# Reordering the frequency-domain products by time block, and accumulating the inverse transforms per frequency half

## The chip, the core and the metric

The kernel runs on one core of one Trainium2 chip. The metric is the device time of one execution in microseconds (us), the median of several runs. A profile of one execution gives, beside this, the span from the first to the last instruction.

## The reference

For one sequence of L = 2048 tokens and D = 512 channels, the output mixes two branches with a gate per token:

```python
g = _sigmoid((x * gate_w).sum(-1, keepdims=True))
a = _A_ref(x, ...)      # state-space convolution, every channel by its own kernel K, plus x * Dskip
b = _B_ref(x, ...)      # x, and for the 2 tokens with the largest x @ w_r a feed-forward part added
return g * a + (1 - g) * b
```

The part that matters here is the convolution in `_A_ref`. It builds a kernel K of 2048 lags per channel and convolves along time by way of spectra:

```python
K = jnp.einsum("dn,dnl,dn->dl", Cc, P, dB).real
Kf = rfft2(pad(K)); Uf = rfft2(pad(up))
Yf = Uf * Kf[None, :, :, :]
y = irfft2(Yf)[:, :, 0, :L] + u * Dskip
```

## The kernel before, in words

The kernel cuts time into two blocks of 1024 tokens and the channels into two halves `h` of 256. All transforms are matrix products on TensorE (PE) with cosine and sine matrices, with 512 frequency pairs in 4 tiles `ft` of 128, a real and an imaginary `part`, and even and odd time steps kept apart (`par` in time, `pm` for the two frequencies that share a cosine). The stages around the change are these.

- `forward` (from L711 on, matmuls L736 and L738) transforms the two time blocks of x into the tile X.
- `kgen(h)` (matmuls L756, L769, L775) makes the convolution kernel of a channel half, and `kspec(h)` (matmuls L791) transforms it into KK[h], kernel block by kernel block, in two halves `qd` of the frequency tiles (tiles 0 and 1, then 2 and 3). ScalarE (ACT) or VectorE (DVE) copies each result out of PSUM (recorded under helper line L402).
- `products(h, qd)` (L797 to L826) multiplies spectra on DVE, all of it tensor-tensor work recorded under helper line L387. For one frequency half it does block 1 and then block 0 (the loop at L811). Block 1 of the output is X1·K0 + X0·K1 and takes six operations on 2048 columns (into the scratch tiles PA, PBb and PC), then four on 1024 columns; block 0 is X0·K0 and takes two on 2048 and four on 1024. Of the four, the first two (L820, L821) write the scratch tile YY, and the last two (L825, L826), here called the closing sums, write the result over X in place, first for pm = 0, then for pm = 1. PA, PBb, PC and YY exist once, so that one unit's operations follow the other's in the order in which the program states them, with only little overlap.
- `inverse(h)` (L830 to L861) goes over block 1, then block 0; in each over `par`, and in that over the time half `t2`. One PE operation is 16 matmuls (L841): two column groups `e` of 8 accumulating matmuls each, over all 4 frequency tiles and both parts, into one of 4 PSUM buffers of one bank. It therefore needs the products of both frequency halves. For h = 0, and for block 1 of h = 1, ACT scales the result by the gate into YA (two operations, recorded under L398), and after the second t2 one DVE operation of 1024 columns adds YA to U (L852, recorded under L387). For block 0 of h = 1, DVE does both in one operation per column group (L857, recorded under L394). After a block, four DMAs on the queue of SyncE (SP) write 128 KB each to the output (L860, recorded under L409).

The main program states these steps in this order: `kspec(0)`, `kgen(1)`, `products(0, 0)`, `products(0, 1)`, the load of the inverse matrices G (L898), `kspec(1)`, `inverse(0)`, `products(1, 0)`, `products(1, 1)`, `inverse(1)` (L894 to L903).

The order on each engine is not the order of the program text. `Prog.schedule` (L107) is a planner: among all operations whose predecessors are planned it takes the one with the earliest start, and among equals the one with the longest remaining path (`key = (st, -o.bl - o.prio)`, L143), with costs that the program gives each operation. Each engine then runs its list strictly in that order and waits on semaphores. A copy out of PSUM that may go to ACT or DVE (`EV`) is put on the one that the planner expects to be done first.

Of the kernel before, what the change touches and what calls it, by code (L numbers as in the profile page):

```python
# [13 lines left out]
ACTF = mybir.ActivationFunctionType  # L14
# [3 lines left out]
PE, ACT, DVE, POOL, SP = "pe", "act", "dve", "pool", "sp"  # L18
# [9 lines left out]
def dr(a, off, *dims):  # L28
    return bass.AP(a.tensor, off, [[s, c] for (s, c) in dims])
# [225 lines left out]
L, D, NS, NF = 2048, 512, 128, 1792  # L255
BLK, NBLK, HF, HC = 1024, 2, 2, 256
# [70 lines left out]
def bass_gated_mix__ssm_conv_s4__moe_arch_mod__prompt_kernel(nc, A_u, A_A_re, A_A_im, A_B_re, A_B_im, A_C_re, A_C_im, A_log_dt, A_Dskip,  # L327
# [24 lines left out]
    with ExitStack() as es:  # L352
# [25 lines left out]
        def nel(ap):  # L378
            r = 1
            for s, c in ap.ap[1:]:  # L380
                r *= c
            return r
        def tt_cost(o, a, b):
            fast = all(x.dtype == BF for x in (o, a, b)) and all(str(x.tensor.name).startswith("AR") for x in (a, b))
            return 0.157 + nel(o) * (0.52e-3 if fast else 1.04e-3)
        def TT(o, a, b, op, rd, wr, **k):
            return P.op(DVE, lambda h: h.tensor_tensor(out=o, in0=a, in1=b, op=op), rd, wr, cost=tt_cost(o, a, b), **k)  # L387
# [5 lines left out]
        def STT(o, a, sc, b, op0, op1, rd, wr, **k):  # L393
            return P.op(DVE, lambda h: h.scalar_tensor_tensor(out=o, in0=a, scalar=sc, in1=b, op0=op0, op1=op1), rd, wr, cost=0.16 + nel(o) * 1.25e-3, **k)  # L394
        def CP(o, a, rd, wr, **k):
            return P.op(DVE, lambda h: h.tensor_copy(o, a), rd, wr, cost=0.16 + nel(o) * 0.8e-3, **k)
        def AC(o, a, func, rd, wr, scale=1.0, bias=0.0, **k):
            return P.op(ACT, lambda h: h.activation(out=o, in_=a, func=func, scale=scale, bias=bias), rd, wr,  # L398
                        cost=0.185 + nel(o) * 0.833e-3 + (0.09 if not isinstance(scale, float) else 0), **k)
# [8 lines left out]
        def DMA(pairs, rd, wr, nbytes, eng=SP, **k):  # L408
            return P.op(eng, lambda h: [h.dma_start(o, i) for o, i in pairs], rd, wr, cost=0.5 * len(pairs), n=len(pairs), nbytes=nbytes, dma=True, **k)  # L409
# [12 lines left out]
        U = B("u", oA, 16 * KB)  # L422
        X = B("x", oB, 32 * KB)
        P.bufs.remove(X)
        XB = [[B("x%d%d" % (h_, k_), oB + (16 * h_ + 8 * k_) * KB, 8 * KB) for k_ in range(2)] for h_ in range(2)]
        xk = lambda h_, k_, *key: (XB[h_][k_], key)
# [26 lines left out]
        G = B("g", oF + 16 * KB, 16 * KB)  # L453
# [114 lines left out]
        MUL, ADD, SUB = ALU.mult, ALU.add, ALU.subtract  # L568
# [225 lines left out]
                        o = KK[h](0, 128, i * 4096 + part * 2048 + 2 * qd * 256, (1024, 2), (1, 512))  # L794
                        EV(o, pb(0, 128, 0, (512, 2), (1, 512)), [pb.buf], [(KK[h], (i, part, qd))])

        def products(h, qd):  # L797
            def xv(blk, part=None, pm=None):
                o = h * 8192 + blk * 4096 + 2 * qd * 256
                if part is None:  # L800
                    return X(0, 128, o, (2048, 2), (1024, 2), (1, 512))
                if pm is None:
                    return X(0, 128, o + part * 2048, (1024, 2), (1, 512))
                return X(0, 128, o + part * 2048 + pm * 1024, (1, 512))
            def kv(blk, part):
                return KK[h](0, 128, blk * 4096 + part * 2048 + 2 * qd * 256, (0, 2), (1024, 2), (1, 512))
            v4 = lambda b: b(0, 128, 0, (1024, 2), (512, 2), (1, 512))
            v1 = lambda b, part: b(0, 128, part * 1024, (1, 1024))
            kx = lambda blk: [xk(h, blk, part, pm, ft) for part in range(2) for pm in range(2) for ft in (2 * qd, 2 * qd + 1)]
            kk = lambda blk, part: [(KK[h], (blk, part, qd))]  # L810
            for blk in (1, 0):  # L811
                TT(v4(PA), xv(blk), kv(0, 0), MUL, kx(blk) + kk(0, 0), [PA])
                if blk == 1:
                    TT(v4(PC), xv(0), kv(1, 0), MUL, kx(0) + kk(1, 0), [PC])
                    TT(PA(0, 128, 0, (1, 2048)), PA(0, 128, 0, (1, 2048)), PC(0, 128, 0, (1, 2048)), ADD, [PA, PC], [PA])
                TT(v4(PBb), xv(blk), kv(0, 1), MUL, kx(blk) + kk(0, 1), [PBb])
                if blk == 1:
# [12 lines left out]
        def inverse(h):  # L830
            for blk in (1, 0):
                for par in range(2):
                    for t2 in range(2):
                        pb = ivb[ni[0] % 4]
                        ni[0] += 1
                        def iv(hh, blk=blk, par=par, t2=t2, pb=pb):
                            last = None
                            for e in range(2):
                                for c in range(8):
                                    part, ft = c % 2, c // 2  # L840
                                    last = hh.matmul(pb(0, 128, e * 256, (1, 256)), G(0, 128, ((par * 2 + part) * 4 + ft) * 512 + (2 * t2 + e) * 128, (1, 128)),  # L841
                                                     X(0, 128, h * 8192 + blk * 4096 + part * 2048 + (par * 4 + ft) * 256, (1, 256)), start=(c == 0), stop=(c == 7))
                            return last
                        P.op(PE, iv, [G] + [xk(h, blk, part, par, ft) for part in range(2) for ft in range(4)], [pb.buf], cost=16 * 0.11)
                        if h == 0 or blk == 1:
                            for e in range(2):
                                tb = blk * 8 + (2 * t2 + e) * 2 + par
                                AC(YA(0, 128, (2 * t2 + e) * 256 + par * 1024, (1, HC)), pb(0, 128, e * 256, (1, HC)), ACTF.Copy, [pb.buf, (SG, "g")], [(YA, (par, t2, e))], scale=SG(0, 128, 32 + tb, (1, 1)))
                            if t2 == 1:
                                tbs = [blk * 8 + s_ * 2 + par for s_ in range(4)]  # L850
                                u = U(0, 128, (blk * 8 + par) * D + h * HC, (2 * D, 4), (1, HC))
                                TT(u, u, YA(0, 128, par * 1024, (HC, 4), (1, HC)), ADD, [(YA, (par, a_, e)) for a_ in range(2) for e in range(2)] + [(U, ("x", tb)) for tb in tbs], [(U, ("o", tb, h)) for tb in tbs])  # L852
                            continue
                        for e in range(2):
                            tb = blk * 8 + (2 * t2 + e) * 2 + par
                            u = U(0, 128, tb * D + h * HC, (1, HC))
                            STT(u, pb(0, 128, e * 256, (1, 256)), SG(0, 128, 32 + tb, (1, 1)), u, MUL, ADD, [pb.buf, (SG, "g"), (U, ("x", tb))], [(U, ("o", tb, h))])  # L857
                for st in range(4):
                    tb = blk * 8 + st * 2
                    DMA([(dr(out, (1024 * blk + 256 * st) * D + h * HC, (2 * D, 128), (D, 2), (1, HC)), U(0, 128, tb * D + h * HC, (D, 2), (1, HC)))],  # L860
                        [(U, ("o", tb, h)), (U, ("o", tb + 1, h))], [], 131072, tag="final")  # L861
# [31 lines left out]
        tab2(1, (1, 1))  # L893
        kspec(0)  # L894
        kgen(1)
        products(0, 0)
        products(0, 1)
        DMA([(G(0, 128, 0, (1, 8192)), g_c[:, :])], [], [G], 2097152)  # L898
        kspec(1)
        inverse(0)  # L900
        products(1, 0)
        products(1, 1)
        inverse(1)  # L903

        P.span = P.schedule()
# [45 lines left out]
```

## Time and profile before

| | |
|---|---|
| time, median of 3 runs | 206.42 us (206.23 to 206.93) |
| span of the profiled execution | 203.5 us |
| median less span | 2.9 us |
| PE busy | 163.9 us (81%) |
| DVE busy | 171.3 us (84%) |
| ACT busy | 141.1 us (69%) |
| mean granted PE clock | 0.921 |

The page gives the profiled execution by its span; its own whole time is not listed apart from the three runs. Where a step below is worked out on the span, it is carried over to the median as a difference. Busy shares are means over stages with different limits, so the stage that holds the change, from about 150 us to the end, is to be read by itself: which engine waits there, and for whom.

### The profile page before, as it was taken

Reading aid. Unit: us, or ns where it says so; the run is one execution under the profiler, and the core shown is the slowest. Engines: PE = TensorE matmul, PEld = TensorE weight load, DVE = VectorE, ACT = ScalarE, POOL = GpSimd, SP = SyncE. Lnnn points to the kernel's source line nnn. Section 1 sums busy time; section 2 is a strip of 40 time slices with the busy share of each in tenths; the row PEclk is TensorE's granted clock in tenths of the full one; section 3 lists DMA queues with packets and bytes.
Section 4 is the critical chain, followed back from the end, with each engine's and each line's share of the span. In section 5 each row is a group of like instructions: output and inputs, shape, how many; then the busy total and the mean of one; then the engine's idle time right before and its main releaser. Section 6 shows DMA issues by size and latency. Waiting matters only on the chain.

```text
span 203.5 us, 3609 instructions
## 1 busy us (share of the span) xinstructions
PE 163.9 (81%) x1479; PEld 108.6 (53%) x1490; DVE 171.3 (84%) x281; ACT 141.1 (69%) x232; POOL 3.4 (2%) x7
## 2 busy tenths in 40 slices
PE   0084799999999999999984999509889999809992
PEld 0073544774344444466550387408668888607881
DVE  0579545699999999999489999999999999999152
ACT  2599999989999999699999946406636654401400
POOL 6000000000000000000000000000000000000000
PEclk9997579999999999999997599966999999985998
DMA  5998999149202022000498000000280000303033
GB/s 86 271 323 364 307 410 358 33 121 293 53 0 55 0 52 52 0 3 0 135 435 362 0 5 0 0 0 3 61 354 0 3 0 0 106 0 103 0 103 103
DMA packets 22097, 23.17 MB, mean 114 GB/s; under 512 B 13121, under 2 KB 19394, under 8 KB 21442
## 3 DMA queue, kind: packets, MB, share of 16 engines
q1 hardware_dynamic: 20738, 22.63, 33.8%
q10 hardware_dynamic: 1344, 0.33, 1.4%
q8 instruction: 11, 0.18, 0.4%
q14 instruction: 4, 0.03, 0.0%
HBM read 19.02 MB, written 3.15 MB: 109 GB/s over the span
## 4 chain that ended last, share of the span: by engine, by line
PE 63%; DVE 22%; ACT 7%; DMA 4%; issue 1%; SPq 1%; DVEq 0%
PE ps L736 28%; DVE AR L387 20%; PE ps L841 12%; PE ps L791 6%; PE ps L756 5%; ACT AR L402 4%; DMA AR<-in_A_u_dram 4%; PE ps L769 3%; ACT AR L398 3%; PE ps L738 2%; PE ps L711 2%; PE ps L625 1%; PE ps L700 1%; SPq L483 1%; PE ps L637 1%
## 5 line engine op out<-in xcount | busy, mean ns | idle before, releaser
L387 DVE TENSOR_TENSOR AR<-AR 128x1024 bf16<-128x1024 bf16 (+7 forms) x184 | 135.7, 797 | 12.5 <-DMA AR<-in_A_A_re_dram 6.8
L398 ACT ACTIVATE AR<-AR 128x512 bf16<-128x512 f32 (+4 forms) x84 | 59.5, 769 | 5.4 <-DVE AR L391 2.1
L402 ACT ACTIVATE AR<-ps 128x1024 bf16<-128x1024 f32 (+4 forms) x56 | 44.0, 811 | 25.5 <-PE ps L791 12.8
L736 PE MATMUL ps<-AR 128*128 128x512 bf16 x248 | 59.0, 388 | 0.8 <-issue 0.5
L736 PEld LDWEIGHTS ps<-AR 128*128 128x128 bf16 x256 | 25.3, 100 | 30.2 <-issue 2.7
L841 PE MATMUL ps<-AR 128*128 128x256 bf16 x256 | 31.1, 287 | 5.9 <-DVE AR L387 5.9
L398 ACT ACTIVATE AR<-ps,AR 128x256 bf16<-128x256 f32 (+1 forms) x40 | 20.4, 565 | 18.8 <-PE ps L841 18.8
L841 PEld LDWEIGHTS ps<-AR 128*128 128x128 bf16 x256 | 26.3, 103 | 10.2 <-DVE AR L387 6.2
L791 PE MATMUL ps<-AR 128*128 128x256 bf16 x224 | 26.1, 274 | 1.7 <-ACT AR L402 1.7
L791 PEld LDWEIGHTS ps<-AR 128*128 128x128 bf16 x224 | 21.7, 99 | 6.1 <-ACT AR L402 3.1
L406 ACT ACTIVATE AR<-AR 128x256 int32<-128x256 f32 (+1 forms) x50 | 21.1, 484 | 0.1
L756 PE MATMUL ps<-AR 128*128 128x84 bf16 x256 | 13.5, 213 | 7.9 <-DVE AR L387 7.6
L756 PEld LDWEIGHTS ps<-AR 128*128 128x128 bf16 x256 | 12.0, 105 | 11.1 <-DVE AR L387 7.9
L625 PE MATMUL ps<-AR 128*128 128x128 bf16 x64 | 6.3, 278 | 12.5 <-DMA AR<-in_A_u_dram 10.8
L391 DVE TENSOR_SCALAR AR<-AR 128x1024 int32<-128x1024 int32 (+4 forms) x24 | 13.2, 552 | 0.3
L625 PEld LDWEIGHTS ps<-AR 128*128 128x128 bf16 x64 | 5.4, 127 | 13.1 <-DMA AR<-in_A_u_dram 10.8
L402 DVE CAST AR<-ps 128x1024 bf16<-128x1024 f32 (+1 forms) x7 | 8.0, 1142 | 3.2 <-remote 1.7
L867 PE MATMUL ps<-AR 128*128 128x512 bf16 x13 | 6.4, 492 | 3.6 <-ACT AR L398 3.6
L868 PE MATMUL ps<-AR 128*128 128x512 bf16 x16 | 7.6, 474 | 0.2
L406 DVE TENSOR_SCALAR AR<-AR 128x256 int32<-128x256 f32 (+1 forms) x22 | 5.6, 296 | 1.9 <-ACT AR L398 1.8
L769 PE MATMUL ps<-AR 128*32 128x128 bf16 (+1 forms) x96 | 6.4, 383 | 0.5 <-ACT AR L402 0.5
L402 DVE COPY AR<-ps 128x1024 bf16<-128x1024 bf16 (+1 forms) x7 | 4.7, 686 | 1.7 <-PE ps L625 1.4
(36 smaller groups left out, 57.0 us busy)
## 6 DMA issues: line engine op xcount, KB each, us to landing
AR<-c_ksp SPq DMA_DIRECT2D x1, 3584.0 KB, 13.5
AR<-in_A_u_dram SPq DMA_DIRECT2D x2, 1024.0 KB, 8.4
AR<-c_fwd SPq DMA_DIRECT2D x1, 2048.0 KB, 8.0
AR<-c_fwdn SPq DMA_DIRECT2D x8, 256.0 KB, 4.4
AR<-c_inv SPq DMA_DIRECT2D x1, 2048.0 KB, 8.9
out_dram<-AR SPq DMA_DIRECT2D x16, 128.0 KB, 2.2
AR<-in_B_w_gate_dram SPq DMA_DIRECT2D x1, 1792.0 KB, 11.2
AR<-in_B_w_up_dram SPq DMA_DIRECT2D x2, 896.0 KB, 11.5
```

The lines of the kernel that those rows point to most:

```text
L387: return P.op(DVE, lambda h: h.tensor_tensor(out=o, in0=a, in1=b, op=op), rd, wr, cost=tt_cost(o, a, b), **k)
L391: return P.op(DVE, lambda h: h.tensor_scalar(out=o, in0=a, scalar1=s1, scalar2=None, op0=op0), rd, wr, cost=c, **k)
L398: return P.op(ACT, lambda h: h.activation(out=o, in_=a, func=func, scale=scale, bias=bias), rd, wr, cost=0.185 + nel(o) * 0.833e-3 + (0.09 ...
L402: return P.op((ACT, DVE), (lambda h: h.activation(out=o, in_=a, func=ACTF.Copy), lambda h: h.tensor_copy(o, a)), rd, wr, cost=(0.185 + n * ...
L406: return P.op((ACT, DVE), (lambda h: h.activation(out=o, in_=a, func=ACTF.Copy, scale=c), lambda h: h.tensor_scalar(out=o, in0=a, scalar1= ...
L625: last = h.transpose(bb(0, 128, db * 256 + t_ * 128, (1, 128)), U(0, 128, (2 * q + t_) * D + db * 128, (1, 128)), IDN(0, (1, 128)))
L736: last = h.matmul(o, w, U(0, 128, (blk * 8 + st * 2 + par) * D, (1, D)), start=(par + st == 0), stop=(par * 4 + st == 7 and blk == 0))
L756: last = hh.matmul(pb(0, 128, (g - b0) * 84, (1, 84)), TP[h][1 - part](0, 128, g * 128, (1, 128)), TQ[h][1 - part](0, 128, g * 84, (1, 84) ...
L769: last = hh.matmul(pb(32 * g, 32, c4, (256, njg), (4, 64)), lw, KA[h](0, 128, c4 + 4 * (8 * bk + g), (16, njg), (84, 64)), start=True, sto ...
L791: last = hh.matmul(pb(0, 128, n * 256, (1, 256)), KP(0, 128, u * 2048 + tau * 128, (1, 128)), KC[h](0, 128, jg * 256, (1, 256)), start=(k ...
L841: last = hh.matmul(pb(0, 128, e * 256, (1, 256)), G(0, 128, ((par * 2 + part) * 4 + ft) * 512 + (2 * t2 + e) * 128, (1, 128)), X(0, 128, h ...
L868: return h.matmul(pb(0, 128, c0, (1, D)), OHR(0, 128, tb * 128, (1, 128)), ZB(0, 128, D, (1, D)), start=False, stop=True)
```

## The change

Three things are changed.

1. `products(h, qd)` gets the list of blocks as an argument, and the main program calls it for block 1 of both frequency halves first, then for block 0 of both. The operations are the same.
2. In `inverse(h)` each PE operation of 16 matmuls becomes two of 8: `q = 0` accumulates frequency tiles 0 and 1 for all four pairs of `t2` and `par` into the four PSUM buffers, and `q = 1` accumulates tiles 2 and 3 on top. The matmuls are the same in number and shape; each operation now needs only its own frequency half. Only the first matmul into a bank starts a new accumulation.
3. Within a block the loop now goes over the time half `t2` outside and `par` inside, so that the DVE addition covers one time half (four neighbouring token tiles) in place of one parity. The ACT, DVE and DMA operations are the same in number and size.

The core of the diff:

```diff
-        def products(h, qd):
+        def products(h, qd, blks):
...
-            for blk in (1, 0):
+            for blk in blks:
...
             for blk in (1, 0):
-                for par in range(2):
+                bufs = {}
+                for q in range(2):
                     for t2 in range(2):
-                        pb = ivb[ni[0] % 4]
-                        ni[0] += 1
-                        def iv(hh, blk=blk, par=par, t2=t2, pb=pb):
-                            for e in range(2):
-                                for c in range(8):
-                                    part, ft = c % 2, c // 2
-                                    last = hh.matmul(..., start=(c == 0), stop=(c == 7))
-                        P.op(PE, iv, [G] + [xk(h, blk, part, par, ft) for part in range(2) for ft in range(4)], [pb.buf], cost=16 * 0.11)
+                        for par in range(2):
+                            if q == 0:
+                                bufs[t2, par] = ivb[ni[0] % 4]
+                                ni[0] += 1
+                            pb = bufs[t2, par]
+                            def iv(hh, blk=blk, par=par, t2=t2, pb=pb, q=q):
+                                for e in range(2):
+                                    for c in range(4):
+                                        part, ft = c % 2, 2 * q + c // 2
+                                        last = hh.matmul(..., start=(q + e + c == 0), stop=(q == 1 and e == 1 and c == 3))
+                            P.op(PE, iv, [G] + [xk(h, blk, part, par, ft) for part in range(2) for ft in (2 * q, 2 * q + 1)], [pb.buf], cost=8 * 0.11)
+                            if q == 0:
+                                continue
...
-                            if t2 == 1:
-                                tbs = [blk * 8 + s_ * 2 + par for s_ in range(4)]
-                                u = U(0, 128, (blk * 8 + par) * D + h * HC, (2 * D, 4), (1, HC))
-                                TT(u, u, YA(0, 128, par * 1024, (HC, 4), (1, HC)), ADD, ...)
+                                if par == 1:
+                                    tbs = [blk * 8 + 4 * t2 + k for k in range(4)]
+                                    u = U(0, 128, (blk * 8 + 4 * t2) * D + h * HC, (D, 4), (1, HC))
+                                    TT(u, u, YA(0, 128, t2 * 1024, (HC, 4), (1, HC)), ADD, ...)
...
-        products(0, 0)
-        products(0, 1)
+        for blks in ((1,), (0,)):
+            for qd in range(2):
+                products(0, qd, blks)
...
-        products(1, 0)
-        products(1, 1)
+        for blks in ((1,), (0,)):
+            for qd in range(2):
+                products(1, qd, blks)
         inverse(1)
```

More of the change, by code (lines that the diff above doesn't have):

```diff
@@ L831, in inverse @@
             for blk in (1, 0):
-                for par in range(2):
+                bufs = {}
+                for q in range(2):
                     for t2 in range(2):
-                        pb = ivb[ni[0] % 4]
-                        ni[0] += 1
-                        def iv(hh, blk=blk, par=par, t2=t2, pb=pb):
-                            last = None
-                            for e in range(2):
-                                for c in range(8):
-                                    part, ft = c % 2, c // 2
-                                    last = hh.matmul(pb(0, 128, e * 256, (1, 256)), G(0, 128, ((par * 2 + part) * 4 + ft) * 512 + (2 * t2 + e) * 128, (1, 128)),
-                                                     X(0, 128, h * 8192 + blk * 4096 + part * 2048 + (par * 4 + ft) * 256, (1, 256)), start=(c == 0), stop=(c == 7))
-                            return last
-                        P.op(PE, iv, [G] + [xk(h, blk, part, par, ft) for part in range(2) for ft in range(4)], [pb.buf], cost=16 * 0.11)
-                        if h == 0 or blk == 1:
+                        for par in range(2):
[4 more added lines that the diff above has]
+                            def iv(hh, blk=blk, par=par, t2=t2, pb=pb, q=q):
+                                last = None
+                                for e in range(2):
+                                    for c in range(4):
+                                        part, ft = c % 2, 2 * q + c // 2
+                                        last = hh.matmul(pb(0, 128, e * 256, (1, 256)), G(0, 128, ((par * 2 + part) * 4 + ft) * 512 + (2 * t2 + e) * 128, (1, 128)),
+                                                         X(0, 128, h * 8192 + blk * 4096 + part * 2048 + (par * 4 + ft) * 256, (1, 256)), start=(q + e + c == 0), stop=(q == 1 and e == 1 and c == 3))
+                                return last
+                            P.op(PE, iv, [G] + [xk(h, blk, part, par, ft) for part in range(2) for ft in (2 * q, 2 * q + 1)], [pb.buf], cost=8 * 0.11)
+                            if q == 0:
+                                continue
+                            if h == 0 or blk == 1:
+                                for e in range(2):
+                                    tb = blk * 8 + (2 * t2 + e) * 2 + par
+                                    AC(YA(0, 128, t2 * 1024 + (2 * e + par) * 256, (1, HC)), pb(0, 128, e * 256, (1, HC)), ACTF.Copy, [pb.buf, (SG, "g")], [(YA, (par, t2, e))], scale=SG(0, 128, 32 + tb, (1, 1)))
+                                if par == 1:
+                                    tbs = [blk * 8 + 4 * t2 + k for k in range(4)]
+                                    u = U(0, 128, (blk * 8 + 4 * t2) * D + h * HC, (D, 4), (1, HC))
+                                    TT(u, u, YA(0, 128, t2 * 1024, (HC, 4), (1, HC)), ADD, [(YA, (p_, t2, e)) for p_ in range(2) for e in range(2)] + [(U, ("x", tb)) for tb in tbs], [(U, ("o", tb, h)) for tb in tbs])
+                                continue
@@ L846, in inverse @@
                             for e in range(2):
                                 tb = blk * 8 + (2 * t2 + e) * 2 + par
-                                AC(YA(0, 128, (2 * t2 + e) * 256 + par * 1024, (1, HC)), pb(0, 128, e * 256, (1, HC)), ACTF.Copy, [pb.buf, (SG, "g")], [(YA, (par, t2, e))], scale=SG(0, 128, 32 + tb, (1, 1)))
-                            if t2 == 1:
-                                tbs = [blk * 8 + s_ * 2 + par for s_ in range(4)]
-                                u = U(0, 128, (blk * 8 + par) * D + h * HC, (2 * D, 4), (1, HC))
-                                TT(u, u, YA(0, 128, par * 1024, (HC, 4), (1, HC)), ADD, [(YA, (par, a_, e)) for a_ in range(2) for e in range(2)] + [(U, ("x", tb)) for tb in tbs], [(U, ("o", tb, h)) for tb in tbs])
@@ L853, in inverse @@
[L853 to L857, printed above, removed]
+                                u = U(0, 128, tb * D + h * HC, (1, HC))
+                                STT(u, pb(0, 128, e * 256, (1, 256)), SG(0, 128, 32 + tb, (1, 1)), u, MUL, ADD, [pb.buf, (SG, "g"), (U, ("x", tb))], [(U, ("o", tb, h))])
```

## The prediction, made before the changed kernel was run

> **What bounds the kernel now.** The page comes first, for the span and for the slices in which an engine is not full.
>
> ```profile
> span 203.5 us, 3609 instructions
> PE   0084799999999999999984999509889999809992
> DVE  0579545699999999999489999999999999999152
> PEclk9997579999999999999997599966999999985998
> ```
>
> A slice is 5.09 us. DVE is full from slice 23 to slice 36 and nearly empty in the last three. PE is full through slice 34, falls to 0 in slice 35 (178 to 183 us), and is full again to the end, in slice 36 at a clock of 0.5. So PE stands idle for DVE, restarts slowly, and is then the only full engine. The chain of waits for the last stretch and the table of waits say the same:
>
> ```profile
> 166.71 3.51 PE ps L841 x32
> 173.04 9.99 DVE AR L387 x12
> 183.08 16.68 PE ps L841 x128
> 199.78 0.48 DVE AR L394
> PE ps L841 <- DVE AR L387: 5.9, 1, 5.9
> ```
>
> All 128 inverse matmuls of the second channel half (`inverse(1)`) begin at 183.08, when DVE has block 1 complete in both frequency halves, and run without a break to 199.76. The end follows from them. A table of windows gives what each piece holds (window and length, then busy us and counts of PE, weight loads, DVE, ACT and POOL, then the granted PE clock):
>
> ```profile
> 116.70:188.56 71.86, 55.88 (x562) 46.53 (x561) 71.56 (x94) 31.69 (x49) 0.00 (x0) 0.90 0.13 45
> 150.40:177.20 26.80, 26.55 (x240) 23.33 (x240) 26.65 (x32) 13.63 (x22) 0.00 (x0) 1.00 0.13 46
> 177.20:181.40 4.20, 0.00 (x0) 0.00 (x0) 4.20 (x6) 0.84 (x2) 0.00 (x0) 1.00 0.00 0
> 181.40:183.10 1.70, 0.02 (x1) 0.03 (x2) 1.70 (x4) 0.00 (x0) 0.00 (x0) 0.52 0.00 0
> 183.10:188.30 5.20, 5.20 (x25) 3.73 (x26) 5.13 (x7) 0.84 (x2) 0.00 (x0) 0.50 0.35 101
> 188.30:199.80 11.50, 11.45 (x105) 10.01 (x103) 4.28 (x10) 2.52 (x6) 0.00 (x0) 1.00 0.16 46
> 183.54:188.56 5.02, 5.02 (x27) 3.64 (x26) 4.94 (x7) 0.84 (x2) 0.00 (x0) 0.53 0.36 104
> ```
>
> DVE is busy 71.56 of 71.86 us up to 188.56, when the last product is done. That makes it the bound up to there; PE's own work before (the last of `inverse(0)`) ends at 177.20. What follows is 16.7 us of PE, of which only the first 5.5 lie beside DVE work.
>
> **The change part by part.**
>
> *Products in a new order.* Nothing is added or removed on DVE, and with no idle time to fill, the products cannot end before about D = 188.6. What moves is what is done last. In the order of the program the second channel half goes block 1 and block 0 of frequency half 0, then of frequency half 1. The last unit, block 0 of frequency half 1, is the window 183.54 to 188.56: two long and four short operations in 5.0 us. The other unit of block 0, of the same six shapes, costs the same 5.0 us and now stands ahead of block 1's second half; the change puts it behind. Without any interleaving block 1 would be complete at 188.6 - 2 x 5.0 = 178.6, not at 183.6.
>
> The planner interleaves, though. Among operations ready together it takes the longest remaining path, and a unit's closing sums become ready with the next unit's first multiplications, which have more behind them. Two rows give the paces:
>
> ```profile
> L387 DVE TENSOR_TENSOR AR<-AR 128x2048 bf16<-128x2048 bf16 x32 | 38.1, 1218 | 0.1
> L387 DVE TENSOR_TENSOR AR<-AR 128x1024 bf16<-128x1024 bf16 x44 | 28.3, 684 | 0.1
> 182.94 3.68 DVE L387 TENSOR_TENSOR AR<-AR 128x1024 bf16<-128x1024 bf16 x4
> 185.93 1.29 DVE L387 TENSOR_TENSOR AR<-AR 128x1024 bf16<-128x1024 bf16 x2
> ```
>
> Durations overlap a little. Two short ones take 1.29, so the pace of a short one is 1.29 - 0.68 = 0.6; short, long, long, short take 3.68, so the pace of a long one is (3.68 - 0.6 - 0.68)/2 = 1.2, or 1.14 without the stall between dependent ones. I go back from D in the order that the planner's rule gives: last two closing sums 1.2; the two YY operations 1.2; closing sums of block 0, frequency half 0, 1.2; the last two multiplications 2.3; two YY 1.2; closing sums of block 1, frequency half 1, 1.2. So the sums of block 0's first half end at 186.2 (pm = 0 at 185.6) and those of block 1's second half at 181.4 (pm = 0 at 180.8). I take these late values; without interleaving they would be 183.6 and 178.6.
>
> *Inverse per frequency half.* At full clock one matmul takes its step from this row (PE only, the 96 matmuls that end `inverse(0)`):
>
> ```profile
> 166.70:177.20 10.50, 10.49 (x96) 1.00 0.18 52
> ```
>
> 10.49/96 = 0.109 us, so 32 matmuls, one frequency half of one block, take 3.5 us, and all 128 take 14.0. PE then goes: block 1's first half, whose products ended some 10 us earlier, from 177.2 to 180.7; its second half from 180.8 (closing sum) to 184.3; block 0's first half from 185.6 (closing sum) to 189.1; block 0's second half, ready at 188.0 for pm = 0, from 189.1 to 192.6. The last wait is 1.3 us, and 16.7 becomes 14.0 because the slow restart goes: 25 matmuls took 5.20 us at clock 0.50, or 0.208 each, against 0.109, which is 2.5 us. In the rows above the clock fell only 4.2 us after PE had stopped. The four PSUM buffers are taken again by block 0 in the order in which block 1's second half leaves them; ACT empties one in this time, next to 0.88 for 8 matmuls:
>
> ```profile
> 163.69 0.84 ACT L398 ACTIVATE AR<-ps,AR 128x256 bf16<-128x256 f32 x2 [0.68 <-PE ps L841]
> ```
>
> The first is free at about 180.8 + 0.88 + 0.84 = 182.5, before 185.6: no wait.
>
> A rule speaks against short groups of matmuls. The row is 150.40 to 177.20: there too PE worked in groups that waited for ACT and changed PSUM buffers, idle 0.25 of 26.80 us, and the clock stayed 1.00. The Trainium skill, page "TensorE: Matmul & The Clock Gate", section "A second HAM failure mode: psum-queue depth-cycling", says that cycling PSUM banks lets PE idle briefly so often that the clock swings between half and full. By that rule the tail would lose part of the 2.5 us and more; by the row it loses nothing. I go by the row and keep the rule as a rival.
>
> *Finish by time half.* Counts and shapes are kept, so durations are too. What moves is when DVE adds. In `inverse(1)` the two additions for block 1 (0.6 each) came after the products; now their inputs are ready at about 183.5 and 185.3, while DVE still multiplies. Where DVE would wait for a dependent operation, the planner slips a ready one in. I take one ahead of the last sums (D = 189.2) and one behind: nothing on the path, as PE reaches block 0's second half only at 189.1. Both ahead of block 0's first closing sums would cost 1.2; none would give D = 188.6 and no gain, as PE's sum above does not touch it. For an addition planned too early, the multiplications queued behind it on DVE would wait with it, and PE behind these.
>
> *The end.* Behind the last matmul stand one pair of DVE operations and the last output DMAs:
>
> ```profile
> 199.78 0.88 DVE L394 SCALAR_TENSOR_TENSOR AR<-ps,AR 128x256 bf16<-128x256 f32 x2 [0.87 <-PE ps L841]
> 198.55 2.94 SPq L409 DMA_DIRECT2D out_dram<-AR  x4
> ```
>
> From 199.76 to 203.5 that is 3.7 us, and it stays: the last pair still releases the last two of the four DMAs on SP's queue. The four pairs before fit beside 8 matmuls each (0.88 against 0.88).
>
> *The first channel half.* DVE does the same work there, without a gap to fill. PE has `kspec(1)` to do meanwhile, and ACT's copies of it feed the second half's products:
>
> ```profile
> AR<-c_inv SPq DMA_DIRECT2D x1, 2048.0 KB, 8.9
> 145.40 0.32 SPq L409 DMA_DIRECT2D AR<-c_inv  x1
> 163.65 3.06 PE ps L791 x28
> 165.88 1.94 ACT L402 ACTIVATE AR<-ps 128x1024 bf16<-128x1024 f32 x2 [1.34 <-PE ps L791]
> ```
>
> G lands at 145.4 + 8.9 = 154.3, so no inverse matmul starts earlier than before (`inverse(0)` began near 157). The pieces of 8 fill PE's gaps between `kspec(1)` groups more finely, and the first four hand nothing to ACT. The last copy of KK[1] lands at 165.88 + 1.94 = 167.8; block 1's second frequency half, now needed earlier, starts at about D - 2 x 5.0 - 9.6 = 169 (9.6 being 5.0 and four long ones more), so it finds its input, with 1 us to spare and some 2 more until the part that came last is used. I take 0; the bounds are 0 and 3.
>
> **Sum.** 192.6 + 3.7 = 196.3 against 203.5, so -7.2 us; 206.42 - 7.2 = 199.2. The bounds: if closing sums are not held back, block 0's second half waits only for D, its first sum at 188.0 plus 3.5 is 191.5, and the time is 198.1; with both additions ahead of the sums it is 200.4. The forecast's own range is 198.1 to 200.6.
>
> **The rivals.**
>
> *Block 0's first half does not run ahead* (its sums are put last, or PE's list has it behind). Then all 64 matmuls of block 0 come after the last sums, from 188.6 (D = 189.2) to 195.6: 199.3, a time of 202.2. For it: the planner may hold sums back. Against: they start PE work. 0.12.
>
> *DVE waits at the seam of the channel halves*, for KK[1] or an addition planned too early, by 1 to 3 us: 200.2 to 202.2. For it: the 1 us to spare above. 0.07.
>
> *The clock falls anyway.* At 0.208 a matmul, the last 64 take 13.3 in place of 7.0, for 205.5; the last 96 take 20.0 in place of 10.5, for 208.7: about even. For it: 1.3 us of wait in my own sum. Against: the row with clock 1.00. The Trainium skill's section on depth-cycling, above, is the rule that speaks for it. I give it 0.03, counted as no change, with another 0.01 that the DVE order stays as it was.
>
> *Slower: inverse matmuls stand ahead of `kspec(1)` in PE's list.* PE takes its list strictly in order. With the 96 matmuls that now follow the last `kspec(1)` group set ahead of it, KK[1] would be complete at 167.8 + 10.5 = 178.3, DVE would wait for it from about 169, 9.3 us, and the time would be 208.5. It decides at 7.2 us of such waiting. For it: the halves are ready sooner than the whole operations were. Against: `kspec(1)` has the longer path behind it and the planner prefers it; before, the inverse only filled its gaps. 0.04.
>
> **How the numbers follow.** Forecast 0.73, the rivals as above. With the first two rivals 0.92 lies between 198.1 and 202.2; I take 197.8 to 202.3. A measurement here can tell about 0.3%, 0.6 us, from no change. Faster: 0.73 + 0.12 + 0.07, rounded to 0.93; same 0.03; slower 0.04.
>
> **What would show it.** In the profile after: PE's wait for DVE at L841 under 2 us in all after 150 us, a clock of 1.00 from 150 to the end of PE, DVE without a gap to about 189, PE's end near 192.6, and 3.7 us behind it. It is wrong if DVE shows a gap behind ACT or PE near 160 to 170, if 64 matmuls stand behind the last product, or if the clock falls after 177.

## The result, and the profile after

| | before | after |
|---|---|---|
| time, median | 206.32 us (206.17 to 206.93, 4 runs) | 200.61 us (199.98 to 201.14, 4 runs) |
| span of the profiled execution | 203.5 us | 198.3 us (its own time: 200.09 us) |
| mean granted PE clock | 0.921 | 0.944 |

The ratio is 0.972, with a 95% interval of 0.9684 to 0.9756: 5.7 us less. The forecast was 199.2 us, 7.2 us less than before; the measured time lies within its range.

The lines of the page that answer to those shown of before, the span and the three rows by slices (now 4.96 us each):

```profile
span 198.3 us, 3623 instructions
PE   0074599999999999999996499950988999999791
DVE  0659635599999999999768999999999999999983
PEclk9999759999999999999999759996699999999998
```

In the last nine slices PE has no empty slice any more, only a 7 where it waits for a moment, and the clock stays at 9 up to the last slice. DVE is now full until two slices before the end. The chain of waits for the last stretch and the two rows of the table of waits:

```profile
166.46 3.51 PE ps L845 x32
169.99 0.85 ACT AR L398 x2
170.86 15.87 DVE AR L387 x20
186.77 4.67 PE ps L845 x40
191.47 3.10 DVE AR L394 x7
PE ps L845 <- DVE AR L387: 1.1, 1, 1.1
DVE AR L394 <- PE ps L845: 0.5, 1, 0.5
```

Before, 16.7 us of PE stood alone at the end of the chain. Now DVE stands on it for 15.9 us, PE for 4.7, and DVE again for 3.1. The windows, with columns as before (DVE's full stretch, PE from `kspec(1)` on, its one long wait, the rest of PE, and what lies behind PE):

```profile
121.25:190.93 69.68, 58.59 (x609) 50.02 (x610) 69.47 (x90) 32.34 (x53) 0.00 (x0) 0.95 0.15 50
151.90:185.67 33.77, 33.53 (x304) 29.58 (x304) 33.63 (x41) 16.45 (x30) 0.00 (x0) 1.00 0.15 49
185.67:186.77 1.10, 0.00 (x2) 0.01 (x1) 1.10 (x3) 1.10 (x4) 0.00 (x0) 1.00 0.40 119
186.77:194.05 7.28, 7.28 (x64) 6.09 (x64) 6.74 (x13) 0.00 (x0) 0.00 (x0) 1.00 0.25 72
194.05:198.30 4.25, 0.00 (x0) 0.00 (x0) 0.91 (x3) 0.00 (x0) 0.00 (x0) 0.79 0.43 123
```

PE works from 151.90 to 194.05 with one long wait, of 1.10 us, and the clock at 1.00 throughout. To compare the two traces without what came earlier, take as a mark the start of `kgen(1)`'s 128 matmuls on PE, which wait for DVE in both kernels. First the row of before, then that of after:

```profile
137.56 7.81 PE L756 MATMUL ps<-AR 128*128 128x84 bf16 x128 [7.60 <-DVE AR L387]
```

```profile
139.05 7.81 PE L756 MATMUL ps<-AR 128*128 128x84 bf16 x128 [7.60 <-DVE AR L387]
```

From the mark to the end of PE it is 199.76 - 137.56 = 62.20 us before and 194.05 - 139.05 = 55.00 after: -7.20 us, the forecast's own figure. The span is shorter by only 5.2 because two other pieces grew: the mark lies 1.49 us later, and from the end of PE to the end of the span it is 4.25 us in place of 3.8. The experiments had to say which part of the change brought the 7.2, and where the rest went.

### The profile page after: what moved, and what is told of

The parts are those of the page before. It is cut to its first block, busy times and chain, and to the rows that moved or that the text cites. A ratio compares the mean times of both kernels' runs of the same rounds, so it can differ in the third digit from the quotient of the medians.

```text
span 198.3 us, 3623 instructions
## 1 busy us (share of the span) xinstructions
PE 162.3 (82%) x1490; PEld 106.5 (54%) x1490; DVE 170.9 (86%) x281; ACT 140.8 (71%) x232; POOL 3.4 (2%) x7
## 4 chain that ended last, share of the span: by engine, by line
PE 61%; DVE 19%; ACT 11%; DMA 4%; SPq 1%; issue 1%; DVEq 0%
PE ps L736 29%; DVE AR L387 17%; PE ps L791 7%; ACT AR L398 5%; ACT AR L402 5%; PE ps L845 5%; PE ps L756 5%; DMA AR<-in_A_u_dram 4%; PE ps L769 3%; PE ps L738 2%; PE ps L873 2%; PE ps L711 2%; DVE AR L394 2%; PE ps L625 1%; PE ps L874 1%; PE ps L700 1%
## 5 line engine op out<-in xcount | busy, mean ns | idle before, releaser
L736 PE MATMUL ps<-AR 128*128 128x512 bf16 x256 | 61.3, 391 | 0.0
L736 PEld LDWEIGHTS ps<-AR 128*128 128x128 bf16 x256 | 25.3, 100 | 30.7 <-issue 3.4
L845 PE MATMUL ps<-AR 128*128 128x256 bf16 x256 | 28.7, 273 | 1.1 <-DVE AR L387 1.1
L791 PE MATMUL ps<-AR 128*128 128x256 bf16 x224 | 26.0, 274 | 1.7 <-ACT AR L402 1.7
L845 PEld LDWEIGHTS ps<-AR 128*128 128x128 bf16 x256 | 24.9, 98 | 4.5 <-DVE AR L387 1.6
L791 PEld LDWEIGHTS ps<-AR 128*128 128x128 bf16 x224 | 21.7, 99 | 6.1 <-ACT AR L402 3.1
L756 PEld LDWEIGHTS ps<-AR 128*128 128x128 bf16 x256 | 11.9, 105 | 11.2 <-DVE AR L387 7.9
L625 PEld LDWEIGHTS ps<-AR 128*128 128x128 bf16 x64 | 5.1, 124 | 13.5 <-DMA AR<-in_A_u_dram 11.3
L873 PE MATMUL ps<-AR 128*128 128x512 bf16 x16 | 7.3, 455 | 4.5 <-ACT AR L398 4.5
L874 PE MATMUL ps<-AR 128*128 128x512 bf16 x16 | 7.4, 465 | 0.0
```

The lines of the kernel that those rows point to most:

```text
L625: last = h.transpose(bb(0, 128, db * 256 + t_ * 128, (1, 128)), U(0, 128, (2 * q + t_) * D + db * 128, (1, 128)), IDN(0, (1, 128)))
L736: last = h.matmul(o, w, U(0, 128, (blk * 8 + st * 2 + par) * D, (1, D)), start=(par + st == 0), stop=(par * 4 + st == 7 and blk == 0))
L756: last = hh.matmul(pb(0, 128, (g - b0) * 84, (1, 84)), TP[h][1 - part](0, 128, g * 128, (1, 128)), TQ[h][1 - part](0, 128, g * 84, (1, 84) ...
L791: last = hh.matmul(pb(0, 128, n * 256, (1, 256)), KP(0, 128, u * 2048 + tau * 128, (1, 128)), KC[h](0, 128, jg * 256, (1, 256)), start=(k ...
L873: h.matmul(pb(0, 128, c0, (1, D)), IDN(0, (1, 128)), U(0, 128, tb * D, (1, D)), start=True, stop=False)
```

## The experiments

All were timed beside the kernel before in the same session, whose median was 206.02 us (order alone, halves alone, PE kept at work, after again), 206.14 (before again, the first of the two runs ended by time half, eight buffers, finished partly by ACT) and 206.15 (the others). The stretch is the time from the mark to the end of PE, the tail that from there to the end of the span, both from the profile.

| kernel | time, us | against before | stretch, us | tail, us |
|---|---|---|---|---|
| before, again | 205.79 | -0.35 | 62.4 | 3.8 |
| product order alone | 202.58 | -3.4 | 58.0 | 3.8 |
| frequency halves alone | 200.24 | -5.8 | 56.0 | 4.25 |
| before, PE kept at work | 203.67 | -2.35 | 59.7 | 3.8 |
| after, again | 200.74 | -5.3 | 55.0 | 4.25 |
| after, third time | 199.86 | -6.3 | 55.0 | 4.25 |
| after, ended by time half | 199.28 and 199.17 | -6.9, -7.0 | 55.0 | 3.8 |
| halves alone, ended by time half | 200.03 | -6.1 | 56.0 | 3.8 |
| halves, eight buffers | 199.27 | -6.9 | 54.8 | 4.7 |
| the same, finished partly by ACT | 200.07 | -6.1 | 54.8 | 4.8 |
| the same as eight buffers, two priorities | 198.50 | -7.65 | 54.5 | 3.8 |

### Which part brings the gain

**Product order alone.** The inverse stays as it was before; only the products are called block by block.

```diff
-        products(1, 0)
-        products(1, 1)
+        for blks in ((1,), (0,)):
+            for qd in range(2):
+                products(1, qd, blks)
```

(The same for h = 0.)

> The products go block by block, the inverse stays in operations of 16 matmuls over all four frequency tiles. Theory (the gain is the end of PE's wait plus the end of its slow restart, and either part of the change gives a share of it): block 1 is complete some 2 to 5 us earlier, PE starts the second channel half then, its wait is about 3 to 4 us in place of 5.9, and block 0's 64 matmuls (7.0 us) all come after the last closing sums: about -4 us, 202.3. Rival A (the order carries the whole gain): about -5.7 us, 200.6. Rival B (the order without halves gives nothing, because PE still waits for both frequency halves): 0 to -1.5 us.

Measured: 202.58 us, a ratio of 0.9825 (0.9793 to 0.9856). The timeline of PE in this kernel, the idle time and its releaser in brackets:

```profile
168.24 10.64 PE L841 MATMUL ps<-AR 128*128 128x256 bf16 x96
181.50 7.16 PE L841 MATMUL ps<-AR 128*128 128x256 bf16 x64 [2.62 <-DVE AR L387]
190.04 7.16 PE L841 MATMUL ps<-AR 128*128 128x256 bf16 x64 [1.38 <-DVE AR L387]
```

Block 1 starts after 2.62 us of wait, block 0 after another 1.38, and all 64 matmuls of block 0 stand behind the last product. The stretch is shorter by 4.2 us, as the theory had it; neither rival holds. The time is shorter by 3.4 only; where the rest may have gone is shown below, with the head of the span.

**Frequency halves alone.** The changed kernel, with `products(h, 0, (1, 0))` and `products(h, 1, (1, 0))` in the old order.

> The inverse works in frequency halves and ends by time half, the products keep the old order. Theory: block 1's first half fills 3.5 us of PE's wait after 177.2, the wait left is about 2.4 us, too short for the clock to fall, and the 96 matmuls after it take 10.5 us: PE ends near 193.6 where it ended at 199.8, so -5.7 us, 200.6, nearly as much as both parts together. Rival A (the order carries the gain): 0 to -2 us. Rival C (short groups of matmuls let the clock fall): a granted clock well under 1.00 after 177 us and less than -3 us.

Measured: 200.24 us, 0.9707 (0.9677 to 0.9738), no different from the whole change. Its PE timeline:

```profile
166.36 15.88 PE L845 MATMUL ps<-AR 128*128 128x256 bf16 x144
184.08 10.65 PE L845 MATMUL ps<-AR 128*128 128x256 bf16 x96 [1.84 <-DVE AR L387]
```

Of the 144 matmuls before the wait, 32 are block 1's first half, ahead of time. The wait left is 1.84 us, and the remaining 96 take 10.65. So the two parts are two remedies for the same wait: 4.2 and 6.2 us of stretch alone, 7.2 together. The halves are enough for the time: the new order shortens the stretch by another 1.0 us, but it seems to lose 0.6 to 1.1 us ahead of the mark (below). The third part of the change, the loop over the time half, is in every kernel with halves and was not tried alone.

**PE kept at work.** The kernel before, with 48 matmuls on constants behind the first channel half:

```diff
+        def keep_warm(hh):
+            last = None
+            for n in range(48):
+                last = hh.matmul(fwp[0](0, 128, 0, (1, 256)), G(0, 128, n * 128, (1, 128)), G(0, 128, n * 128, (1, 256)), start=(n == 0), stop=(n == 47))
+            return last
+        kw = P.op(PE, keep_warm, [G], [fwp[0].buf], cost=48 * 0.11)
+        kw.deps.add(lastiv[0].idx)
```

(Not shown: `inverse` notes its last PE operation in `lastiv[0]`.)

> The kernel before, with 48 matmuls on constants into a PSUM buffer that nothing reads, put behind the last matmul of the first channel half, so that PE works through most of its wait for DVE (5.3 of 5.9 us). Nothing else moves. Theory: the wait stays, the restart is at full clock, and 128 matmuls take 14.0 in place of 16.7 us: -2.5 us, 203.8. Rival (the slow stretch is PE sharing memory with DVE's products, not the clock after a pause): 0.

Measured: 203.67 us, 0.9875 (0.9843 to 0.9907), so -2.35 us. PE's timeline, and the window of the second channel half:

```profile
177.51 5.40 PE L905 MATMUL ps<-AR 128*128 128x256 bf16 x48
183.56 14.15 PE L842 MATMUL ps<-AR 128*128 128x256 bf16 x128 [0.65 <-DVE AR L387]
```

```profile
183.56:197.72 14.16, 14.15 (x128) 12.44 (x128) 9.33 (x15) 3.35 (x8) 0.00 (x0) 1.00 0.26 75
```

PE still starts only when DVE releases it, yet the 128 matmuls take 14.15 us in place of 16.68, beside the same DVE work. The slow stretch of before was the clock after the pause, and it was worth 2.5 us; memory shared with DVE is ruled out as its cause. About a third of the stretch that the change saves is clock; the rest is PE starting earlier.

### Where the rest of the forecast went

**The changed kernel again, and before again.**

> The changed kernel again, beside the others on one chip. Theory: 200.6, -5.7 us, and a span of which everything up to the first frequency-domain product varies by 1 to 1.5 us from run to run (load of the input, phase of the clock windows), since no instruction up to there is in another order than before. Rival: the change itself delays the start of the products, by 1.5 us in every run.

> The kernel before, profiled once more, to see how much its part ahead of the change varies. So far its first frequency-domain product began at 119.8 us, and at 120.2 in the run with extra matmuls; in the kernels with a changed order or changed inverse it began at 121.0 to 121.5. Theory (phase of the clock windows and of the input load, nothing of the change): this profile may show any value from 119.8 to 121.5, and time less span stays near 1.8 us. Rival (the changed kernels start the products later in every run): again close to 120.

Measured: 200.74 us, 0.973 (0.9695 to 0.9764), and 205.79 us, 0.9983 (0.9963 to 1.0003). The profile of before has its first product at 119.5 and the mark at 137.28 this time, which is what the rival expected, and again a span of 203.5; but the spans of its 12 runs reach from 203.3 to 204.9, so both profiles of it are among its shortest executions. The time is 1.8 us above the span in both kernels (205.31 to 203.5, 200.37 to 198.6), so the table's 2.9 us of median less span before the change was partly a short execution. Neither expectation is quite right, though. In all six profiles with the new product order DVE waits before its first product, for ACT's copy of KK[0]; here the changed kernel and its second profile:

```profile
121.25 2.16 DVE L387 TENSOR_TENSOR AR<-AR 128x2048 bf16<-128x2048 bf16 x3 [0.47 <-ACT AR L402]
```

```profile
121.52 1.83 DVE L387 TENSOR_TENSOR AR<-AR 128x2048 bf16<-128x2048 bf16 x2 [0.78 <-ACT AR L402]
```

These waits are 0.47 to 0.82 us long. In the eight profiles with the old order there is none in five, and 0.22 to 0.35 in three. My expectation that no instruction up to there stands in another order was wrong: the planner now puts token updates (two matmuls each, L873 and L874) in another order ahead of `kspec(0)`, and ACT's scaling of them with it. ACT then waits for these matmuls, here in the changed kernel:

```profile
115.17 0.69 ACT L398 ACTIVATE AR<-ps,AR 128x512 bf16<-128x512 f32 x1 [0.55 <-PE ps L874]
116.02 0.69 ACT L398 ACTIVATE AR<-ps,AR 128x512 bf16<-128x512 f32 x1 [0.17 <-PE ps L874]
```

All six profiles with the new product order have these two waits, 0.7 us together, and none of the eight with the old order has them. So about 0.6 us of the later mark belongs to the change; that these waits are what delays the copy was not tried by itself. It may be more: the first product begins at 121.2 us on average over the six profiles and at 120.1 over the eight, 1.1 us apart. The rest of the 1.49 us is within what the profiles with the old order show among themselves (marks from 137.28 to 138.76).

**Ended by time half.** In the changed kernel the loop goes over the time half outside, but the planner put both operations of parity 0 first, as they also stood in the kernel before. A priority puts the time half first in the list (only the end of the statement is shown):

```diff
-  ... [pb.buf], cost=8 * 0.11)
+  ... [pb.buf], cost=8 * 0.11, prio=0.5 if q == 1 and t2 == 0 else 0.0)
```

> The changed kernel, with the last operations of the inverse put in the order of the time halves by a priority (both parities of a time half before the next; the planner had put parity first). Theory: the first two of the last four output DMAs start some 0.9 us earlier, so that the four no longer queue up behind one another, and the end comes 0.4 to 0.5 us sooner: 200.2. Rival (the last DMA, not the queue ahead of it, sets the end): 0.

> The changed kernel with the last inverse operations by time half once more, now beside the changed kernel itself on one chip. Theory: 0.4 to 0.5 us less than the changed kernel in the same session, from the output DMAs. Rival (the 1.4 us between the medians of two sessions is real): 1 us or more.

> The changed kernel a third time, as the base for the three others. Theory: 0.97 of the kernel before, 200.4 to 200.8. Rival: 199.5 or less, if its median varies between sessions by as much as the time-half order seemed to bring.

Measured: 199.28 us, 0.9672 (0.9642 to 0.9702), then 199.17, 0.9681 (0.9647 to 0.9715), beside 199.86, 0.9723 (0.969 to 0.9756), for the changed kernel in the same session as the second (expected 200.4 to 200.8). The difference there is 0.7 us, and the intervals overlap. The traces say it more exactly: the stretch is the same 55.0, and the tail falls from 4.25 to 3.8. The last four output DMAs on SP's queue, first of the changed kernel, then with the time half first:

```profile
193.73 2.52 SPq L409 DMA_DIRECT2D out_dram<-AR  x4
```

```profile
193.14 2.94 SPq L409 DMA_DIRECT2D out_dram<-AR  x4
```

Each of these DMAs writes two neighbouring token tiles, one of each parity. With parity first, none can go before the third pair of DVE operations. All four DMAs are then issued in one row, 2.52 us for four, from 193.73, and the last issue ends at 196.25; the last DVE operation had ended at 194.97. The kernel before had parity first too: its first of the four also began with the third pair, at 198.55. But there the pairs stood apart, here the third of before and then all four of after:

```profile
198.04 0.88 DVE L394 SCALAR_TENSOR_TENSOR AR<-ps,AR 128x256 bf16<-128x256 f32 x2 [0.87 <-PE ps L841]
```

```profile
191.47 3.50 DVE L394 SCALAR_TENSOR_TENSOR AR<-ps,AR 128x256 bf16<-128x256 f32 x8 [0.54 <-PE ps L845]
```

A pair came every 1.75 us or so before, as PE did 16 matmuls for each; now the four follow one another, 0.88 us each, while two issues take some 1.2 us. So before, the first two DMAs had gone ahead when the last pair came (four in 2.94 us, the last issue ending 0.8 us after DVE, against 1.3 in the changed kernel). With the time half first they go ahead again: four in 2.94 us. The same priority on the halves alone:

> Frequency halves with the old product order, and the last inverse operations by time half. Theory: the frequency halves carry the gain and the order of the last operations adds 0.4 to 0.5 us: 199.8. Rival (the gain of the time-half order in the changed kernel came from something else, or was scatter): 200.2.

Measured: 200.03 us, 0.9703 (0.9682 to 0.9724), where without it the ratio was 0.9707. The tail falls by the same 0.45 us in the profile, but the medians do not show it; at this size they settle nothing, and I rest on the traces.

### What bounds the end now

**Eight buffers.** Halves with the old product order, and block 0 of the second channel half accumulated in the four PSUM banks that `kspec` no longer needs:

```diff
-  bufs[t2, par] = ivb[ni[0] % 4]
+  bufs[t2, par] = (ivx if h == 1 and blk == 0 else ivb)[ni[0] % 4]
```

(Not shown: `ivx`, the list of these four.)

> The frequency halves with the old product order, and four more PSUM buffers for block 0 of the second channel half, so that its first half can run while block 1's second half still waits for DVE. Theory: PE then has 64 matmuls for the wait, works from the end of the first channel half to its own end with no wait over 0.5 us, and is bound by DVE's last sums plus 3.5 us: about 2 us less than the halves alone at PE's end, but DVE has two additions and four pairs to do after its last product, 4.5 us, so 0.8 to 1.5 us less in time, 199.0 to 199.5. Rival (PE's rate, not its order, bounds the end): same as the halves alone, 200.2.

Measured: 199.27 us, 0.9675 (0.964 to 0.9709). The time is as expected, the way to it is not: PE ran 64 matmuls ahead and still waited. PE, then DVE, in this kernel:

```profile
185.45 7.16 PE L846 MATMUL ps<-AR 128*128 128x256 bf16 x64 [0.94 <-DVE AR L387]
189.15 0.69 DVE L387 TENSOR_TENSOR AR<-AR 128x1024 bf16<-128x1024 bf16 x1 [0.50 <-ACT AR L398]
190.43 0.68 DVE L387 TENSOR_TENSOR AR<-AR 128x1024 bf16<-128x1024 bf16 x1
191.03 2.83 DVE L394 SCALAR_TENSOR_TENSOR AR<-ps,AR 128x256 bf16<-128x256 f32 x7
```

With more buffers the planner saw less work behind block 1's closing sums and put two multiplications ahead of them, and DVE's two additions now stand among the last pairs.

**Finished partly by ACT.** As eight buffers, with `if h == 0 or blk == 1 or t2 == 0:` at the branch to ACT, and the time half first.

> As the kernel with eight buffers, and block 0's first time half of the second channel half is scaled by ACT and added by DVE in one operation, as block 1 is, with the last inverse operations in the order of the time halves. DVE then has 3.5 in place of 4.5 us to do after its last product, and the last DMAs queue less. Theory: 0.5 to 1 us less than with eight buffers alone, 198.3 to 198.8. Rival: 0, if PE's end sets the time alone.

Measured: 200.07 us, 0.971 (0.9682 to 0.9737): no gain over eight buffers alone, against the expectation. The median is 0.8 us above theirs, but the intervals overlap; in the profiles the stretch is the same 54.8 and the tail 0.2 us longer. DVE's timeline shows why nothing was won:

```profile
190.59 0.69 DVE L387 TENSOR_TENSOR AR<-AR 128x1024 bf16<-128x1024 bf16 x1 [0.77 <-ACT AR L398]
192.34 0.48 DVE L394 SCALAR_TENSOR_TENSOR AR<-ps,AR 128x256 bf16<-128x256 f32 x1 [1.06 <-PE ps L846]
192.75 0.68 DVE L387 TENSOR_TENSOR AR<-AR 128x1024 bf16<-128x1024 bf16 x1
```

DVE has less to do but waits 0.77 and 1.06 us for ACT and PE, and the addition that releases the first two DMAs falls between the last pairs, so all four issue late.

**Eight buffers and two priorities.** The time half first, and:

```diff
-  TT(sd(0), y(0), y(1), ADD, [YY], kw(0))
+  TT(sd(0), y(0), y(1), ADD, [YY], kw(0), prio=5.0 if h == blk == 1 else 0.0)
```

(The same for `sd(1)`.)

> The kernel with frequency halves, old product order and eight buffers, with two priorities more: block 1's last closing sums go ahead of the multiplications behind them, and the last inverse operations go by time half. Theory: with eight buffers alone PE still stood 0.94 us at 185.45, because the planner had put two multiplications (2.3 us) ahead of the sums that PE waited for. Without this wait PE runs from the first channel half to its end without a break, ends 1 us sooner, and the last DMAs start sooner: 1.5 to 2 us less than with eight buffers alone, 197.3 to 197.8. Rival (DVE's rest after its last product bounds the end by itself): 0 to -0.5 us, 198.8 to 199.3.

Measured: 198.50 us, 0.9631 (0.9599 to 0.9664), the lowest median of all, with an interval that lies wholly below that of the changed kernel. It is 0.8 us below eight buffers, from another session and with overlapping intervals; against the kernel with the time half first the intervals overlap as well. PE, then DVE:

```profile
165.44 22.87 PE L846 MATMUL ps<-AR 128*128 128x256 bf16 x208
188.82 3.67 PE L846 MATMUL ps<-AR 128*128 128x256 bf16 x32 [0.51 <-DVE AR L387]
189.91 3.50 DVE L394 SCALAR_TENSOR_TENSOR AR<-ps,AR 128x256 bf16<-128x256 f32 x8
```

The theory's order came about (208 matmuls without a break), but its size did not: PE's end gained only 0.2 us over eight buffers, since one addition slipped ahead of the last sums and PE waited 0.51 us for them; most of what the span gained, 0.9 us, is the tail. DVE is now without a pause from its products to its last pair, and PE all but so: what is left is work, not waiting.

## Why the prediction was right, and where it was off

- **The bound and the sum.** PE's idle time for DVE, the slow restart and the 128 matmuls at the end were the right three terms. PE's end was put at 192.6 on the clock of the trace before; measured, it is 194.05 with the mark 1.49 us later, 192.56. The terms hold one by one: the last 64 matmuls took 7.28 us (two halves of 3.5 forecast; 64 without a break take 7.16 in product order alone, so 0.1 was wait), the last wait 1.10 (1.3), and the restart was worth 2.5, as the kernel kept at work shows.
- **The closing sums held back.** The order by which the planner puts them behind the next multiplications came as worked out: PE waits for block 0's first sums and continues at 186.77. Without this term the forecast would have been 1 us lower.
- **The additions.** Both slipped ahead of the last sums, not one. The last sum ended at 190.93, where the forecast's D = 189.2, moved by the 1.49 us of the mark, gives 190.7. Both stood behind block 0's first sums, for which PE waited, and not ahead of them, where the forecast priced them at 1.2 us; so they cost PE next to nothing, 0.1 us, because it was at work on block 0's first half until then.
- **The step that failed** is "the end": "From 199.76 to 203.5 that is 3.7 us, and it stays". It measured 4.25. The last pair still released the last two of the four DMAs, as the text says; but it took the pairs to stand as far apart as before. They now follow one another every 0.88 us in place of 1.75, two issues take some 1.2 us, and so the last two were queued behind the first two. Parity first, the planner's choice in both kernels, left no earlier moment for the first two; the order of the loop, by time half, would have. That is 0.5 us.
- **The step that was missing** is the head: "The first channel half. DVE does the same work there" looked at `kspec(1)` only. A new order of products changes path lengths, and with them the planner's list before the first product; 0.6 us of wait came of that, and up to 1.1 us by the means of all profiles. Together -7.2 + 0.5 + 0.6 = -6.1, or -5.6 with 1.1; the three sessions gave -5.7, -5.3 and -6.3 us and do not tell the two apart.
- **The rivals.** Block 0's first half did run ahead; the seam of the channel halves showed no wait (DVE is busy 69.47 of 69.68 us); the inverse did not get ahead of `kspec(1)`, though in this kernel its pieces of 8 went into the gaps. The clock did not fall. The Trainium skill, page "TensorE: Matmul & The Clock Gate", section "A second HAM failure mode: psum-queue depth-cycling", describes a kernel with such cycling of banks whose clock swung; the trace does not agree here: with groups of 8 matmuls that change banks each time, and a wait of 1.10 us, the granted clock was 1.00 from 151.90 to 194.05.
- **What was not seen.** The forecast gave the sum over both parts and never asked what each would give alone. Its own rows had the answer: 183.1 + 96 x 0.109 = 193.6 for PE's end with the halves alone, 1 us above the forecast for both.

## What to carry to other kernels

When an engine waits for a producer and then does all its work in one piece, splitting its work by what is ready and reordering the producer are two remedies for one wait: price each alone before adding them up, since here 4.2 and 6.2 us made 7.2. Count a cold restart as part of the wait; it is won as soon as the wait is short (here 2.62 us left the clock alone, 5.9 did not). Where a planner sets the order, a change in one stage alters ties elsewhere: look at the list of each engine, the DMA queue's too, ahead of and behind the change, and set a priority where the order matters, which here brought 0.5 us of tail for no work at all.

## What the runs showed of the hardware

In the profile of before, PE's clock fell 4.2 us after PE had stopped and came back 5.2 us after the restart. These are not fixed sizes: in its second profile it was about 4.5 and 5.5 us, as these rows show (PE stops at 177.03 and restarts at 182.93):

```profile
177.03:181.50 4.47, 0.01 (x1) 0.00 (x0) 4.47 (x6) 0.84 (x2) 0.00 (x0) 1.00 0.00 0
181.60:182.93 1.33, 0.00 (x0) 0.00 (x1) 1.33 (x4) 0.00 (x0) 0.00 (x0) 0.50 0.00 0
182.93:188.30 5.37, 5.37 (x26) 3.84 (x27) 5.30 (x7) 0.84 (x2) 0.00 (x0) 0.50 0.34 98
188.45:199.73 11.28, 11.28 (x103) 9.86 (x101) 4.02 (x8) 2.52 (x6) 0.00 (x0) 1.00 0.16 47
```

Waits of 1.1, 1.84 and even 2.62 us left the clock untouched; for the last, in product order alone, it was 1.00 on both sides of the wait:

```profile
142.50:181.50 39.00, 34.46 (x380) 29.15 (x377) 38.83 (x47) 20.64 (x36) 0.00 (x0) 1.00 0.20 69
181.50:197.20 15.70, 14.32 (x128) 12.36 (x128) 12.25 (x20) 3.36 (x8) 0.00 (x0) 1.00 0.23 67
```

A DMA of 128 KB costs its queue about 0.6 us of issue (four in 2.52 us), so the number of DMAs that become ready close together at the end is a term of the sum. And executions of one and the same kernel differ in their span by up to 1.6 us in the 12 runs of the kernel before (203.3 to 204.9) and by 2.2 in the six of the changed kernel run again (197.5 to 199.7), while the stretch from the mark to PE's end was 55.0 us in all three profiles of the changed kernel, with spans of 198.3, 198.6 and 197.8; in the two profiles of before, where the clock changed at another moment, it was 62.2 and 62.4. One profile of each kernel can't settle a difference of 1 us in the span; the distance between two marks in each can, down to some 0.3 us.
